# Identity and two pairs of q, k through SyncE; unit-matrix products that write PSUM with a step; table copies and a row read moved

## The chip, the cores and the metric

The kernel runs on one core of a Trainium2 chip. The metric is the device time of one execution in microseconds; the time given is the median of several runs. The core's engines are TensorE (PE: products, results to PSUM), VectorE (DVE), ScalarE (ACT), GpSimd (POOL) and SyncE (SP, which here only issues transfers). Each engine works its instructions off in the order of its own list and waits on semaphores in front of one whose operands aren't there. SyncE, ScalarE and GpSimd issue the DMA transfers.

## The reference

Windowed attention with eight global keys (4 batches, 8 heads, 768 positions, head width 64), then a block that mixes with two Fourier transforms, normalises and applies a two-layer perceptron:

```python
scores = scale * np.matmul(q, k.transpose(0, 1, 3, 2))
is_global = pos[None, :] < 8
is_local = (rel >= 0) & (rel < 96)
bias = -slopes[:, None, None] * dist[None, :, :]
a = softmax(where(is_global | is_local, scores + bias, -1e9))
attn = np.matmul(a, v)                       # 4 x 8 x 768 x 64
x = attn.transpose(0, 2, 1, 3).reshape(4, 768, 512)

mixed = np.real(fft(fft(x, axis=1), axis=2))
u = x + mixed
un = (u - mean(u)) / sqrt(var(u) + 1e-6)     # over the last axis
out = u + np.maximum(un @ w_ch1, 0.0) @ w_ch2
```

All inputs and the output are float32; the kernel computes in float16 with float32 sums.

## The kernel before

**Order.** The program is written as a list of units, and a planner (class `Plan`, L23) orders them when the kernel is built. Each unit names what it needs, the engine or engines that can do it, and a cost in us. The planner keeps a clock for each engine (`self.t`) and for two DMA streams ("DMA2": the first loads on SyncE and small constants; "DMA": the rest). It always takes the unit that could start first by these clocks; the table `BIAS` shifts chosen units or groups of units forward or back by a fixed number of us. TensorE's units come from four streams (MIX: transforms; ATT: attention; PH and PG: the perceptron's two layers), of which MIX and ATT may be taken up to ten places ahead. What comes out is a fixed order for every engine, and on the chip an engine waits wherever its next instruction is not ready. A queue of GpSimd has at most eight transfers on the way in the plan, as has SyncE's.

**Attention.** Heads are done in pairs, four pairs for a batch (`hp`, pair number n = 4b + hp). `load_qk` (L404) brings q and k of a pair: for batches 0 and 1 GpSimd issues a transfer that converts float32 to float16 on the way (L438); only pair 0 of batch 0 is read as float32 by SyncE (L426, tiles `u`) and converted by ScalarE or VectorE (`cast`, L443). `load_v` (L396) brings v by GpSimd. `trans` (L492) transposes q, then k on TensorE (L507, with the identity `idn` as the moving operand) and VectorE or ScalarE moves the result to `qkT` (L514, L518). `kg_copies` (L468) picks the global keys on GpSimd or VectorE. `score` (L525) makes three groups of scores for a pair; in batches 0 and 1 the distance bias is added by products of the table `dist` with a scaled identity `sid` (L549) ahead of the products of q and k (L559), and ScalarE takes the exponential out of PSUM (L583). Batches 2 and 3 instead multiply by tables `mk`, which ScalarE makes from `dist_k` (L1407); `dist_k` is two GpSimd copies of `dist` (L1403). In those batches q and k are transposed by DMA issued by SyncE (L485). `av` (L663) multiplies by v and normalises (L702, L704) into the tile X[b].

**Mixing.** `fold_0` (batch 0) and `fold_s`, `fold_d` form sums and differences on VectorE, with a scaling on ScalarE in batch 0 (`f5`, L812). `y_unit` (L900, four groups g) and `u_unit` (L985, three units of two row residues) are the two transforms on TensorE, `mirror` (L944) reversed copies on GpSimd. x itself must be added to u in another row order. In batches 1 to 3 `bounce` (L717) writes X[b] to a scratch tensor in DRAM (`xd`) and reads it back by rows (`xr`, L732); ScalarE issues both. In batch 0 `spread` (L988) adds x by 12 products of 64 x 64 tiles for each `u_unit` with shifted parts of a unit matrix (`PX`, L993), straight into the PSUM bank of u, whose columns are ordered by r, then n, where x has n, then r.

**Perceptron.** `nt_unit` (L1101) transposes the normalised rows, `ph_unit` (L1134, L1144) is the first layer, whose results ScalarE or VectorE moves to `hT` (L1150, L1151), `pg_unit` (L1157) the second; the last four tiles (c from 8) use seven products of quarter matrices in place of eight (`pg_units`, L1242). The rows leave by SyncE (L1182, L1345, L1349).

**Start.** The order in which the loads are listed begins at L1356: q and k of pair 0, the identity `ident`, `dist`, `gb` (all SyncE), q and k of pairs 2 and 1, v of pairs 0 and 2, q and k of pair 3, v of pairs 1 and 3, then batch 1 (all GpSimd). Twelve products on a zeroed tile (L1384) run on TensorE while nothing has landed.

Of the kernel before, what the change touches and what calls it, by code (L numbers as in the profile page):

```python
# [22 lines left out]
class Plan:  # L23
# [11 lines left out]
    def __init__(self):  # L35
        self.t = {"PE": 0.0, "ACT": 0.0, "DVE": 0.0, "POOL": 0.0, "SP": 0.7, "DMA": 3.75, "DMA2": 1.9}
        self.tok = {}
        self.ready = []
        self.pending = []
        self.rings = {}  # L40
        self.left = {}
        self.n = 0
        self.lanes = [0.0] * 8
        self.soft = [0.0] * 8
# [64 lines left out]
    def emit(self, place):  # L109
# [8 lines left out]
        if dma:  # L118
            q = "DMA2" if outs and outs[0] in (("ld", 0), ("ld", 1), ("c", "id"), ("c", "dist"), ("c", "gb")) else "DMA"
# [29 lines left out]
    def slot(self, tag):  # L149
# [7 lines left out]
    BIAS = {('mk1', '*', 4): 1.5, ('y', 1, 2, 2, 'r'): -3, ('qk', '*', 2): -0.7, (2, 90): -0.7, ('ob', '*', 2): -0.3,  # L157
            (3, '*', 7): -1.5, ('ex', 2, 2, 0): 1.5, ('ss', '*', 6): 0.3, (0, 20): -3, (1, 57): -0.7, ('mk1', '*', 5): 1.5,
            ('v', '*', 1): 1.5, ('c', 't2'): -0.3, ('mk1', '*', 7): 0.7, ('kG', '*', 1): 0.7, ('z', 1, 0): 3, ('u', 2, 0): 0.7}
# [4 lines left out]
    AQ = (4, 5)  # L164
    ORD = {("qk", 0): 0, ("v", 0): 0, ("qk", 1): 5, "w1": 6, "gate": 7, ("v", 1): 8, "w2": 9, ("qk", 2): 10, ("v", 2): 10, ("qk", 3): 10, ("v", 3): 10}
# [42 lines left out]
def act(n):  # L208
    return 0.06 + n / 1200.0


def dve(n):
    return 0.085 + n / 960.0
# [11 lines left out]
def kernel(  # L225
# [178 lines left out]
    def load_qk(b, hp):  # L404
# [3 lines left out]
        for w, src in enumerate((q, k)):  # L408
# [14 lines left out]
            if n == 0:  # L423
                def read(w=w, rows=rows):
                    t = stage["u", w] = buf("u", w, [P, 2 * NP, 2 * Dh], FP32, 1)
                    nc.sync.dma_start(t, rows)  # L426
                pl.later([("SP", 0.45, read)], [], 0.0, [("ld", w)], lat=1.7, dma=1.35)

                def cast(on, w=w):
                    place()  # L430
                    copy_on(on, qk16[n][:, w].rearrange("p h n t d -> p (h n) (t d)"), stage["u", w])
                pl.later([("ACT", act(768), lambda cast=cast: cast("ACT")), ("DVE", dve(768), lambda cast=cast: cast("DVE"))], [("ld", w)], 0.0,
                         [("qk", 0, w)], [("free", "u", w)], rank=0)
# [58 lines left out]
    def trans(b, hp):  # L492
# [6 lines left out]
        def run(start, ring):  # L499
# [9 lines left out]
            e = pl.pe(0.7, start, True)  # L509
# [15 lines left out]
    def score(b, hp, g):  # L525
# [3 lines left out]
        def run(start, ring):  # L529
# [33 lines left out]
            e = pl.pe(0.25 + 0.21 * pem, start, True)  # L563
# [153 lines left out]
    def bounce(b):  # L717
# [11 lines left out]
        def rd():  # L729
            XR[b] = buf("xr", b, [P, NS, Dm], FP16, 3)  # L730
            rows = XD[b].rearrange("(m r) d -> m r d", r=6)
            eng.dma_start(XR[b], rows)  # L732
        pl.later([("ACT", 0.5, rd)], [("xw", b)] + free("xr", b), 0.0, [("xr", b)], lat=1.7, dma=2.4)
# [58 lines left out]
    def fold_0():  # L792
# [19 lines left out]
        def f5(hp):  # L812
            pm = cell["pm"][:, hp]
            A(z(4, 1, hp)[:, 0], pm[:, 1, 0], AF.Copy, 0.0, c)
            A(z(5, 1, hp)[:, 0], pm[:, 0, 1], AF.Copy, 0.0, c)
# [19 lines left out]
        for x in range(2):  # L835
            for hp in (x, x + 2):
# [4 lines left out]
                pl.later([("ACT", 2 * act(128), lambda hp=hp: f5(hp))], [("f2", 0, hp)], 0.0, [("f5", 0, hp)], [("free", "ww", 0)], rank=0)  # L841
# [143 lines left out]
    def u_unit(b, pr):  # L985
        c = NP * b + pr

        def spread(pu):  # L988
            for jj in range(3):
                for a, r in enumerate(PAIRS[pr]):  # L990
                    for h in range(2):
                        t = slice(64 * (r % 2), 64 * (r % 2) + 64)
                        nc.tensor.matmul(pu[64 * h:64 * h + 64, a, :].rearrange("p (r n) -> p r n", r=4), PX[0][t, 3 * (r // 2) + jj],  # L993
                                         X[0][t, 3 * h + jj].rearrange("p (n r) -> p r n", r=4), start=(jj == 0), stop=False,
# [11 lines left out]
        def run(start, ring):  # L1006
# [28 lines left out]
            def add():  # L1035
                u = UT[c] = buf("u", c + 2, [P, 2, Dm], FP32, 2)
# [8 lines left out]
            def add1(on, a):  # L1045
                if a == 0:
                    UT[c] = buf("u", c + 2, [P, 2, Dm], FP32, 2)
# [6 lines left out]
            if b:  # L1054
                pl.later([("DVE", 2 * dve(512) + 0.25, add)], [("xr", b)] + free("u", c + 2), e, [("u", c, 0), ("u", c, 1)],
                         [("free", "xr", b)] + CD(b, ring), ring=ring)
            else:
                for a in range(2):
                    pl.later([("DVE", dve(512) + 0.06, lambda a=a: add1("DVE", a)), ("ACT", act(512) + 0.25, lambda a=a: add1("ACT", a))],
                             (free("u", c + 2) if a == 0 else [("us", c, 0)]), e, [("us", c, a)],  # L1060
# [498 lines left out]
```

## Time and profile before

| | |
|---|---|
| median of 5 runs | 263.2 us (262.88 to 266.57) |
| profiled execution | 263.45 us |
| its span, first to last instruction | 261.5 us |
| mean granted TensorE clock | 0.993 |
| PE busy | 246.1 us (94%) |
| DVE, ACT, POOL busy | 163.0, 143.0, 121.3 us |
| GpSimd's DMA queue (converting loads) | 66096 packets, 63.9% of 16 engines' span |
| first DMA queue of the other issuers | 24672 packets, 21.3% |

The page gives each engine's busy time and its share of the span. A timeline line has the start in us, the length, the engine, the line of the kernel, the operation, the tile written and the tiles read, and the number of instructions merged; in square brackets stands the idle time of the engine ahead of it and the work that ended it. A line of a stage has, after the stage's bounds, its length, then the busy time (and number of instructions) of PE, of PE's weight loads, DVE, ACT and POOL, the granted TensorE clock (1.00 is full), the DMA share and GB/s. A line of one source line has the shortest, median and longest duration in ns. SPq, ACTq and POOLq are instructions that issue transfers. A busy TensorE is not one at its peak, as ends of products are modelled.

### The profile page before, as it was taken

What the parts mean: (1) busy time and instruction counts of PE and PEld (TensorE: products, weight loads), DVE (VectorE), ACT (ScalarE), POOL (GpSimd) and SP (SyncE); (2) the same over time, 40 slices, a digit from 0 to 9 for tenths busy, and PEclk for the clock granted to TensorE, in tenths of its full rate; (3) what the DMA queues carried; (4) which work ended last, traced back from release to release, by engine and by line L of the source; (5) the groups of instructions that cost most, each with busy time, mean ns of one, the idle gap of its engine ahead of it and who ended that gap; (6) DMA issues with size and microseconds to landing.
All of it is one profiled execution on the core that took longest, in us unless ns stands there. A gap on an engine that the chain in (4) does not pass through costs nothing.

```text
span 261.5 us, 6774 instructions
## 1 busy us (share of the span) xinstructions
PE 246.1 (94%) x2824; PEld 178.9 (68%) x2824; DVE 163.0 (62%) x362; ACT 143.0 (55%) x240; POOL 121.3 (46%) x212
## 2 busy tenths in 40 slices
PE   7798879899969999999999999999999999999994
PEld 2576546589748676575477466588779568888883
DVE  1649995536981746712276977788986555625463
ACT  4198887675726697851055834794645236534300
POOL 8697796725928978899930304030304011010000
PEclk9799999999999999999999999999999999999999
DMA  7999999996999999999969941401450340200222
GB/s 166 179 158 175 273 206 119 101 202 85 146 139 228 153 136 142 130 127 119 120 117 166 176 190 39 125 3 43 96 188 0 83 120 0 85 38 3 80 83 80
DMA packets 93630, 31.52 MB, mean 121 GB/s; under 512 B 81664, under 2 KB 89984, under 8 KB 93600
## 3 DMA queue, kind: packets, MB, share of 16 engines
q0 software_dynamic: 66096, 14.18, 63.9%
q1 hardware_dynamic: 24672, 12.19, 21.3%
q10 hardware_dynamic: 2832, 4.72, 6.8%
q8 instruction: 22, 0.36, 0.6%
q14 instruction: 8, 0.07, 0.1%
HBM read 30.95 MB, written 8.65 MB: 151 GB/s over the span
## 4 chain that ended last, share of the span: by engine, by line
PE 53%; POOL 22%; DMA 18%; issue 2%; ACT 1%; DVE 1%; SPq 0%; ACTq 0%; POOLq 0%
PE ph L1144 20%; PE pg L1168 11%; POOL qk L414 10%; DMA qk<-in_q_dram 7%; POOL v L400 5%; PE pgD L1249 5%; PE pgA L1249 4%; DMA v<-in_v_dram 4%; PE pu L1017 4%; DMA hT<-in_k_dram 3%; PE py L914 3%; DMA qk<-in_k_dram 2%; DMA qkT<-qk 2%; POOL hT L438 2%; PE pav L685 2%
## 5 line engine op out<-in xcount | busy, mean ns | idle before, releaser
L1144 PE MATMUL ph<-unT,w 128*128 128x256 f16 x768 | 93.3, 273 | 3.4 <-ACT hT L1150 2.3
L1144 PEld LDWEIGHTS <-w 128*128 128x128 f16 x768 | 73.1, 98 | 16.7 <-issue 5.5
L1150 ACT ACTIVATE hT<-ph 128x512 f16<-128x512 f32 x83 | 48.9, 597 | 47.4 <-PE ph L1144 47.1
L1168 PE MATMUL pg<-w,hT 128*128 128x512 f16 x256 | 61.1, 379 | 0.0
L1168 PEld LDWEIGHTS <-hT 128*128 128x128 f16 x256 | 24.1, 98 | 23.7 <-issue 1.2
L1089 POOL TENSOR_SCALAR sm<-sm 128x2 f32<-128x2 f32 x12 | 3.0, 254 | 57.4 <-ACT un L1082 57.2
L400 POOL DMA_DIRECT2D v<-in_v_dram x32 | 24.7, 820 | 0.7 <-DMA hT<-in_k_dram 0.7
L583 ACT ACTIVATE ex<-sc 128x992 f16<-128x992 f32 (+2 forms) x24 | 20.6, 928 | 7.0 <-DVE qkT L514 5.7
L580 ACT ACTIVATE er<-sc 128x768 f16<-128x768 f32 (+2 forms) x24 | 21.5, 925 | 4.9 <-PE sc L555 4.0
L414 POOL DMA_DIRECT2D qk<-in_k_dram x32 | 21.4, 749 | 5.1 <-DMA qk<-in_k_dram 3.3
L414 POOL DMA_DIRECT2D qk<-in_q_dram x32 | 21.4, 730 | 4.1 <-DMA qk<-in_q_dram 2.4
L1177 DVE SCALAR_TENSOR_TENSOR u<-pg,sm,u 128x512 f32<-128x512 f32 x16 | 12.0, 750 | 18.0 <-PE pg L1168 18.0
L1073 ACT ACTIVATE un<-u,sm 128x512 f16<-128x512 f32 x17 | 11.8, 717 | 19.0 <-DVE sm L1043 17.5
L962 POOL COPY ww<-zy 128x512 f16<-128x512 f16 x16 | 9.7, 633 | 21.6 <-PE py L914 11.9
L595 DVE TENSOR_TENSOR ex<-er,mk 128x768 f16<-128x768 f16 (+2 forms) x24 | 15.8, 679 | 4.2 <-ACT er L580 4.2
L1039 DVE SCALAR_TENSOR_TENSOR u<-pu,xr 128x512 f32<-128x512 f32 x18 | 11.7, 688 | 9.6 <-PE pu L1017 9.6
L1082 ACT ACTIVATE un<-un 128x512 f16<-128x512 f16 x24 | 14.9, 624 | 4.7 <-DMA unT<-un 4.7
L685 PE MATMUL pav<-v,ex 128*128 128x65 f16 x352 | 16.9, 193 | 0.0
L685 PEld LDWEIGHTS <-ex 128*128 128x128 f16 x352 | 15.6, 97 | 0.8 <-issue 0.2
L473 POOL COPY kG<-qkT 64x8 f16<-64x8 f16 x28 | 8.5, 305 | 13.6 <-DMA qkT<-qk 12.6
L931 DVE CAST zy<-py 128x512 f16<-128x512 f32 (+1 forms) x8 | 7.1, 892 | 11.6 <-PE py L914 8.8
L929 ACT ACTIVATE zy<-py 128x1024 f16<-128x1024 f32 (+1 forms) x11 | 9.0, 829 | 9.1 <-PE py L914 6.1
(143 smaller groups left out, 390.3 us busy)
## 6 DMA issues: line engine op xcount, KB each, us to landing
out_dram<-u SPq DMA_DIRECT2D x23, 256.0 KB, 2.1
w<-in_moe_w_ch_dram POOLq DMA_DIRECT2D x8, 512.0 KB, 10.8
v<-in_v_dram POOLq DMA_DIRECT2D x32, 96.0 KB, 6.6
xr<-xd ACTq DMA_DIRECT2D x3, 768.0 KB, 4.5
qk<-in_q_dram POOLq DMA_DIRECT2D x32, 48.0 KB, 3.9
qk<-in_k_dram POOLq DMA_DIRECT2D x32, 48.0 KB, 3.5
xd<-x ACTq DMA_DIRECT2D x4, 384.0 KB, 4.6
hT<-in_q_dram POOLq DMA_DIRECT2D x5, 192.0 KB, 7.4
```

The source lines that it names most:

```text
L400: nc.gpsimd.dma_start(v16[b % 2][64 * t:64 * t + 64, h0:h0 + 2, :, 0:Dh].rearrange("m h i d -> m (h i) d"), v[b, h0:h0 + 2].rearrange("h ( ...
L414: nc.gpsimd.dma_start(qk16[n][64 * t:64 * t + 64, w, :, h], src[b, h0 + h].rearrange("(i m t) d -> t m i d", m=64, t=2)[t])
L580: A(mine(), cut(pa), AF.Exp, 0.0, 0.125)
L583: A(cut(expst[hp][:, :, g * 512:g * 512 + (384 if g == 2 else 512)]), cut(pa), AF.Exp, 0.0, 0.125)
L595: VT(o, mine(), m, op=ALU.mult)
L685: nc.tensor.matmul(o[:, s * 65:(s + 1) * 65], lhsT, v16[b % 2][:, 2 * hp + s, i, 0:65], start=(j < 2 and a == 0), stop=(a == len(ops) - 1) ...
L1082: A(x, x, AF.Square, accum_out=MV[c][:, a, 2:3])
L1144: nc.tensor.matmul(ph[:, a * CH:(a + 1) * CH].rearrange("p (x m) -> p x m", x=2), W1[0][:, d, jb * P:(jb + 1) * P], UNT[c][:, :, d, :], st ...
L1150: pl.later([("ACT", act(512), lambda: A(dst, ph, AF.Relu)), ("DVE", dve(512), lambda: V.tensor_scalar_max(dst, ph, 0.0))], [], e, [("h", c ...
L1168: nc.tensor.matmul(pg, HT[c][:, jb, t * P:(t + 1) * P], W2[0][:, jb, :], start=(jb == 0), stop=(jb == NJ - 1))
L1177: V.scalar_tensor_tensor(UT[c][:, t, :], pg, MV[c][:, t, 3:4], UT[c][:, t, :], op0=ALU.mult, op1=ALU.add)
L1249: nc.tensor.matmul(o, lhs(j), rhs(j), start=(first and j == 0), stop=(j == NK - 1), skip_group_check=True)
```

## The change

- SyncE's list begins with the identity, then q and k of pair 0, `dist`, q and k of pair 2, `gb`. q and k of pair 2 of batch 0 are read as float32 and converted by ScalarE or VectorE, as those of pair 0; GpSimd no longer loads them. The `u` tiles of the tail shift by two numbers more (`U0` = 4), as four of them serve the loads first.
- `spread`: x is now read in its own order (n, then r, contiguous), and the result is written to PSUM with a step of 128 words.
- The two `dist_k` copies wait for the last sum of u's third tile (`("us", 2, 1)`) instead of the last x of batch 0.
- The row read of x (`rd`) is issued by SyncE instead of ScalarE.
- `f5` may run on ScalarE or on VectorE.
- Nine warm-up products instead of twelve.
- The list has the first unit of u after the first two groups of y in all batches (before: ahead of y in batch 0, behind y and the mirror copies in the others).
- The planner has other costs for ScalarE, VectorE, transposes, scores, other first clocks of the two DMA streams, and a new table of biases.

```diff
-        self.t = {..., "SP": 0.7, "DMA": 3.75, "DMA2": 1.9}
+        self.t = {..., "SP": 0.7, "DMA": 6.6, "DMA2": 1.2}
...
-    BIAS = {('mk1', '*', 4): 1.5, ('y', 1, 2, 2, 'r'): -3, ('qk', '*', 2): -0.7, (2, 90): -0.7, ('ob', '*', 2): -0.3,
...
+    BIAS = {('u', '*', 1): -1.5, (1, 63): 0.7, ('w', '*', 2): -0.7, ('un', '*', 0): -1.5, (3, '*', 7): -1.5, ('qkT', 14): -3,
+            ('ex', 0, 3, 1): 0.7, ('qk', 9, 0, 1): -0.3, ('w2', '*', 1): 0.3, ('ld', '*', 1): -1.5, (3, '*', 1): -3, ('xw', 3): -3,
...
+    HW = (0, 2)
+    U0 = 4
...
 def act(n):
-    return 0.06 + n / 1200.0
+    return 0.1 + n / 1180.0
 def dve(n):
-    return 0.085 + n / 960.0
+    return 0.13 + n / 960.0
...
-            if n == 0:
+            if n in pl.HW:
                 def read(w=w, rows=rows):
-                    t = stage["u", w] = buf("u", w, [P, 2 * NP, 2 * Dh], FP32, 1)
+                    t = stage["u", n, w] = buf("u", w + n, [P, 2 * NP, 2 * Dh], FP32, 1)
                     nc.sync.dma_start(t, rows)
...
-            e = pl.pe(0.7, start, True)
+            e = pl.pe(1.0, start, True)
...
-            e = pl.pe(0.25 + 0.21 * pem, start, True)
+            e = pl.pe(0.27 + 0.28 * pem, start, True)
...
-            eng.dma_start(XR[b], rows)
-        pl.later([("ACT", 0.5, rd)], [("xw", b)] + free("xr", b), 0.0, [("xr", b)], lat=1.7, dma=2.4)
+            nc.sync.dma_start(XR[b], rows)
+        pl.later([("SP", 0.5, rd)], [("xw", b)] + free("xr", b), 0.0, [("xr", b)], lat=1.7, dma=2.4)
...
-        def f5(hp):
+        def f5(hp, on):
             pm = cell["pm"][:, hp]
-            A(z(4, 1, hp)[:, 0], pm[:, 1, 0], AF.Copy, 0.0, c)
-            A(z(5, 1, hp)[:, 0], pm[:, 0, 1], AF.Copy, 0.0, c)
+            for i, w in ((4, pm[:, 1, 0]), (5, pm[:, 0, 1])):
+                if on == "ACT":
+                    A(z(i, 1, hp)[:, 0], w, AF.Copy, 0.0, c)
+                else:
+                    V.tensor_scalar_mul(z(i, 1, hp)[:, 0], w, c)
...
-                        nc.tensor.matmul(pu[64 * h:64 * h + 64, a, :].rearrange("p (r n) -> p r n", r=4), PX[0][t, 3 * (r // 2) + jj],
-                                         X[0][t, 3 * h + jj].rearrange("p (n r) -> p r n", r=4), start=(jj == 0), stop=False,
+                        nc.tensor.matmul(pu[64 * h:64 * h + 64, a, :].rearrange("p (r n) -> p n r", r=4), PX[0][t, 3 * (r // 2) + jj],
+                                         X[0][t, 3 * h + jj].rearrange("p (n r) -> p n r", r=4), start=(jj == 0), stop=False,
...
+        dma_const(ident, id_d, 0.3, ("c", "id"))
         load_qk(0, 0)
-        dma_const(ident, id_d, 0.3, ("c", "id"))
         dma_const(dist_sb, dist_d, 0.75, ("c", "dist"))
+        if 2 in pl.HW:
+            load_qk(0, 2)
         dma_const(gb_sb, gb_d, 0.1, ("c", "gb"))
-        load_qk(0, 2)
+        if 2 not in pl.HW:
+            load_qk(0, 2)
         load_qk(0, 1)
...
-        for _ in range(12):
+        for _ in range(9):
             nc.tensor.matmul(pz[:, 0, :], EG[:, 0:P], EG, start=True, stop=True)
...
-                     [("c", "dist")] + ([("ex", 0, 3, 2)] if any((0, hp) in DM for hp in range(HP)) else [("x", 0, 3, 1)]), 0.0, [("dk", t)], rank=3)
+                     [("c", "dist")] + ([("us", 2, 1)]), 0.0, [("dk", t)], rank=3)
...
-            if b == 0:
-                u_unit(b, 0)
-            for g in (0, 1, 2, 3):
+            for g in (0, 1):
+                y_unit(b, g)
+            u_unit(b, 0)
+            for g in (2, 3):
                 y_unit(b, g)
             mirror(b)
-            if b:
-                u_unit(b, 0)
             u_unit(b, 1)
```

## The prediction

> **What bounds the kernel now.** I read the page's busy times first, then TensorE's stages, then the places where it stood still, then the start of each queue. The profiled execution took 263.45 us, of which the span is 261.5; 1.95 us lie around it. The median of the five runs is 263.2, so a sum made against this execution is lowered by 0.25 at the end.
>
> ```profile
> PE 246.1 (94%) x2824; PEld 178.9 (68%) x2824; DVE 163.0 (62%) x362; ACT 143.0 (55%) x240; POOL 121.3 (46%) x212
> ```
>
> TensorE is busy for all but 15.4 us. Stages show where those lie:
>
> ```profile
> 0.00:7.70 7.70, 5.00 (x13) 1.64 (x13) 1.17 (x10) 2.97 (x3) 6.66 (x17) 1.00 0.82 177
> 7.70:50.50 42.80, 36.90 (x749) 25.10 (x750) 31.79 (x102) 32.17 (x47) 34.75 (x55) 0.96 1.68 171
> 50.50:75.50 25.00, 25.00 (x340) 20.29 (x341) 16.61 (x34) 15.27 (x32) 12.74 (x23) 1.00 1.13 140
> 75.50:77.80 2.30, 0.04 (x1) 0.00 (x0) 2.27 (x4) 1.25 (x3) 0.61 (x2) 1.00 2.44 134
> 77.80:258.00 180.20, 179.05 (x1724) 131.89 (x1723) 110.70 (x216) 91.30 (x157) 66.55 (x119) 1.00 0.72 103
> ```
>
> The first pair after the stage is its length and TensorE's busy time. The first 7.70 us hold no useful product (the 5.00 are warm-up products on a zeroed tile). Up to 50.5 another 5.9 us are idle; then TensorE is full to the end, but for one hole of 2.29 us at 75.5 and 1.15 us in 180. So the time is TensorE's work plus the idle time of the first 78 us: whatever takes idle time out there, or work out anywhere, moves the end one for one, as long as data for the later batches keep up. The start, and the hole:
>
> ```profile
> 7.89 0.86 PE L507 MATMUL pt<-ident,hT 128*64 128x128 f16 x24
> 9.14 0.85 PE L507 MATMUL pt<-ident,hT 128*64 128x128 f16 x12 [0.39 <-DMA hT<-in_q_dram]
> 10.22 0.85 PE L507 MATMUL pt<-ident,hT 128*64 128x128 f16 x12 [0.23 <-DMA hT<-in_k_dram]
> ...
> 66.40 1.34 ACTq L725 DMA_DIRECT2D xd<-hT  x2
> 76.15 0.35 ACTq L732 DMA_DIRECT2D xr<-xd  x1
> 76.55 0.74 ACT L1407 ACTIVATE mk<-distk 128x640 f16<-128x640 f16 x1 [4.56 <-DMA xd<-hT]
> ...
> 77.82 1.91 PE L1144 MATMUL ph<-unT,w 128*128 128x256 f16 x16 [2.29 <-ACT hT L1150]
> ```
>
> Pair 0 waits for the identity, pair 2 for its k; and at 72 us ScalarE stands for 4.56 us, its queue held by the row read of x (L732) until the write of x has landed, so no ph bank is emptied and TensorE runs dry.
>
> **1. Row read of x by SyncE.** The issue (0.35 us, three times) leaves ScalarE, and the 4.56 us of waiting go to SyncE. TensorE's 2.29 us hole had no other cause: ScalarE's mk tables and hT evacuations behind it were ready. Gain 2.3. Behind the read on SyncE stand a store of out (73.83 before) and the transposes of qk (78.62, which waited for qk data anyway), so it has 2.5 us of room there. For batch 2 it stands among four transposes that fill SyncE from 139.0 to 148.0; the writes' landing took up to 9.0 us, and a transpose held by it would delay scores of batch 3. TensorE has pg products of earlier rows to run meanwhile, so 0; up to 1 us lost if the cover is gone.
>
> **2. Start: order on SyncE, two loads moved.** By the new list of biases k of pair 0 is issued first (a bias of -1.5 on ("ld", 1)), then identity, q of pair 0, dist, q and k of pair 2, gb, at some 0.5 us each (rows of 0.43 to 0.54). The first load landed for ScalarE at 4.23 before and the second at 5.55; with 64 KB of identity between them, the second would be 5.8, its cast (0.84) ends at 6.65, and the first transposes start there rather than at 7.89: 1.2 earlier. The identity is there at about 4.5, so sid (1.16 us of VectorE) and the sums of ones are done before. Pair 0's scores began at 11.0, because in TensorE's queue pair 2's transposes stood ahead; they now need dist, which landed at 8.8 (issued 2.40, 6.4 to landing).
>
> Pair 2 is the doubtful part. Its k must land on SyncE's queue behind dist. At the pace of the second load behind the first (1.32 us each) it lands at 8.8 + 2.64 = 11.4; cast, transposes (0.86) and evacuation (0.96) bring its first exponential to 14.5, where it was at some 14.7 (ScalarE's six from 12.09 on, 0.84 each). So nothing is lost there and little won. Best case: it lands at 9.4, as the plan's own figures have it (a start of 1.2, four loads at 1.35, identity and dist 1.05, 1.7 to be seen), and the exponentials run on from pair 0's at 9.9 instead of 12.09: 2.2 won. Worst case: identity and dist, 384 KB, took from 5.55 to 8.8, 118 KB per us beside GpSimd's loads; 768 KB at that pace land at 15.3, and the first exponential of pair 2 is at 18.5, 3.8 late.
>
> GpSimd drops two issues (0.83 each) and two converting loads, which landed 1.08 apart (9.13 and 10.21); v and pair 3 come some 2.2 earlier. ScalarE waited 0.62 and 0.18 us for pair 3's scores (at 20.66 and 21.83); those waits go. With 0.2 from pair 2 (14.5 for 14.7) the start gives 1.0; the best case above makes it 3.0, the worst -3.8. Two casts of 0.84 more lie in ScalarE's idle time (6.4 to 12.1); without that cover they cost 1.7.
>
> The Trainium skill (DMA: Bandwidth & Descriptors, "Issuing engines are not separate DMA queues") says that transfers issued by different engines share the same 16 engines, so that another issuer saves only issue time. By it the moved loads would arrive no sooner than before, and the start would keep only the identity's share; no row here shows pair 2 in SyncE's queue.
>
> **3. Tables later.** The dist_k copies held GpSimd from 30.01 to 33.62, with kG copies behind them, for which TensorE waited 0.93 us at 38.54. They go behind u of the third tile (about 50), where GpSimd is idle for 1.71 and 2.07 us; the mk tables need them at 68.3 only. VectorE's last fold ended at 38.63, beside the end of that wait, so I count half: 0.5 (0 to 0.9). If the later place were not free, rstd would be 3.6 late; its first user on VectorE stood at 73.05, so nothing follows.
>
> **4. Products with the unit matrix (L993).** 36 products, nine steps of four at a time. They now read x with a step of four elements:
>
> ```profile
> L993 PE MATMUL pu<-x,er x36: 607/626/646, 31.9 to 47.3; 64*64 64x512 f16 x36
> 44.17 1.35 PE pu L993 x12
> 31.01 0.40 PE L549 MATMUL sc<-dist,sid 64*64 64x496 f16 x4
> ```
>
> A step of four takes 0.45 us (12 in 1.35). Four score products of 496 columns, plain on both sides, took 0.23 (31.01 to the next at 31.24). After the change the read is plain and the write to PSUM has a step of 128 words; no matmul of the trace writes so. If the write is free, nine steps save 9 x 0.22 = 2.0. If it is as slow as the stepped read: 0. VectorE reads PSUM with this very step at 0.69 us for 512 (L1053); at that pace four take 0.69 and nine lose 2.2. I take 0, by the nearest row, the same instruction with one of its sides stepped.
>
> The Trainium skill (PSUM — Partial Sum Buffer, "Specifications (TRN2)") has lines of 8 bytes in PSUM and says that any pattern that isn't contiguous slows matmuls significantly. By it the change gains nothing here or loses; the trace's stepped read shows a factor of two for SBUF, and nothing for PSUM.
>
> **5. The rest.** Three warm-up products fewer (0.43 us apart) end at 4.9 rather than 6.2, in idle time. The records show the clock halved from 9.1 to 12.5 after the idle stretch before 7.7; a longer one could halve pair 0's transposes, 0.86 more: kept for the range. A half of the fold's scaling may go to VectorE (0.3 us each, eight in all), y and u change places in the list, and new costs and biases move the whole order: 0, with 1.5 either way, as the holes of this order (0.2 to 1.1 us each up to 50.5) show what a misplaced item costs.
>
> Sum: 2.3 + 1.0 + 0.5 + 0 = 3.8. 263.45 - 3.8 = 259.65 for such an execution, **259.4** against the median.
>
> **Rivals.**
> (a) The stepped write runs at the plain rate: 2.0 more, 257.4. For it: VectorE's stepped read of PSUM costs no more than its plain one (0.69 for both L1053 and L1151). Against it: 0.69 per 512 is too slow a test for 0.22.
> (b) The hole is closed, the start isn't shortened: pair 2 lands near 13, the casts stand in ScalarE's way, or TensorE waits later for batch 2 or 3, whose loads form the chain from 62.6 to 146. Then 2.3 less about 0.8: 261.7, which is no change.
> (c) Slower: SyncE's share of the DMA engines. k of pair 2 at 15.3 holds all exponentials of batch 0 up by 3.8, since TensorE's and ScalarE's queues are in order, and 2.3 + 0.5 come back: 263.2 + 1.0 = 264.2, with the order's 1.5 up to 265.7. It decides from a landing at 14.4 (11.6 keeps pair 2's old time, 2.8 later eats the other gains). For it: 118 KB per us. Against: the first loads' 1.32 us each, and two loads fewer on GpSimd's queue.
> (d) That the moved loads don't leave GpSimd is excluded: the diff issues them on SyncE.
>
> **How the numbers follow.** Forecast 0.40, (a) 0.28, (b) 0.18, (c) 0.14. A measurement of this kernel can tell about 1% (2.6 us) from no change, that is below 260.6 or above 265.8. The forecast and (a) are below it but for order's 1.5 (0.66 in all, with a little of (b)); (b) and most of (c) lie within: 0.24; a tenth is left above, (c) with a bad order or a slow PSUM write beside it. The likeliest case's own range is 257.9 to 260.9, the order's 1.5 either way; to hold most of (a) with a better start (257.4 less up to 2.0) and (c), the range is 255.8 to 264.5.
>
> **What would show it.** First transposes at 6.6 to 6.8; pair 2's k cast at 11 to 12.5 (at 16: (c)); no wait of ScalarE for xd and no hole near 75; L993 at 12 in 1.35 (0.7: (a); 2 or more: the write is slow); pgl before the y products without GpSimd ahead of it; TensorE full from 48 on. Wrong, if the hole comes back elsewhere, or idle time past 78 us grows by more than 1.5.

## The result, and the profile after

The changed kernel takes 263.91 us (median of 38 runs, 262.38 to 265.61) where the kernel before takes 263.11 (64 runs beside it). The ratio is 1.0036, 95% interval 1.0022 to 1.0050: 0.6 to 1.3 us slower, no gain. The ratios, here and below, leave out executions in a second, slower state, so they differ a little from the quotients of the medians. The profiled execution of the changed kernel took 263.31, its span 261.5, as long as that of before. On the chip SyncE's order is k of pair 0, the identity, q of pair 0, `dist`, q and k of pair 2, `gb`: the biases put k ahead of the identity, and q of pair 0 comes third.

TensorE's busy time (page, part 1), and its stages in the trace of the changed kernel, cut at the same times as before; the first pair is the stage's length and TensorE's busy time, and the last three numbers are the granted clock, the DMA share and GB/s:

```profile
PE 246.9 (94%) x2821; PEld 180.6 (69%) x2821; DVE 167.4 (64%) x374; ACT 139.8 (53%) x234; POOL 119.7 (46%) x206
```

```profile
0.00:7.70 7.70, 4.11 (x17) 1.36 (x17) 2.97 (x21) 2.12 (x2) 6.66 (x17) 1.00 0.86 193
7.70:50.50 42.80, 35.58 (x667) 24.77 (x668) 27.54 (x87) 31.00 (x41) 26.06 (x43) 0.88 1.56 176
50.50:75.50 25.00, 24.59 (x388) 19.50 (x386) 20.12 (x44) 19.66 (x42) 17.37 (x28) 1.00 1.40 188
75.50:77.80 2.30, 2.30 (x20) 1.68 (x18) 1.39 (x3) 1.42 (x3) 2.30 (x4) 1.00 1.05 272
77.80:258.00 180.20, 180.18 (x1739) 133.25 (x1736) 114.79 (x220) 85.62 (x148) 67.33 (x118) 1.00 0.67 95
```

Read them from the bottom. The hole at 75.5 is gone (2.30 busy of 2.30, before 0.04), and of the 1.15 us of idle time behind it 0.02 are left. Yet the span is no shorter: from 7.7 to 50.5 TensorE is busy for 1.32 us less than before, and the work that was not done there comes later. In the first 7.7 us it has 0.89 less, but that is warm-up products. Some of what is busy is also slower: the granted clock of the second stage is 0.88, before 0.96. The first y products begin 4.87 us later (kernel before, then changed kernel):

```profile
38.86 2.14 PE L914 MATMUL py<-t,ww 128*128 128x256 f16 x18
```

```profile
43.73 1.92 PE L922 MATMUL py<-t,ww 128*128 128x256 f16 x16
```

So the hole was closed and the start got longer. The list of ScalarE in time order (start, length, instruction, in brackets the idle time before it and what ended it), and the transposes on TensorE that wait for it:

```profile
3.83 0.84 ACT L448 ACTIVATE hT<-u 128x768 f16<-128x768 f32 x1 [1.82 <-DMA u<-in_k_dram]
8.50 0.84 ACT L448 ACTIVATE hT<-u 128x768 f16<-128x768 f32 x1 [3.83 <-DMA u<-in_q_dram]
11.40 0.84 ACT L448 ACTIVATE hT<-u 128x768 f16<-128x768 f32 x1 [2.06 <-DMA u<-in_q_dram]
13.96 0.84 ACT L448 ACTIVATE hT<-u 128x768 f16<-128x768 f32 x1 [1.72 <-DMA u<-in_k_dram]
14.71 2.64 ACT L588 ACTIVATE ex<-sc 128x992 f16<-128x992 f32 x3
```

```profile
9.39 1.49 PE L512 MATMUL pt<-ident,hT 128*64 128x128 f16 x24 [4.10 <-ACT hT L448]
...
13.30 0.85 PE L512 MATMUL pt<-ident,hT 128*64 128x128 f16 x12
14.86 0.85 PE L512 MATMUL pt<-ident,hT 128*64 128x128 f16 x12 [0.70 <-ACT hT L448]
```

The four casts (L448, before L443) wait for k and q of pair 0, then q and k of pair 2. Pair 0's q is there at 8.50, not at 5.8, so the first transposes start 1.50 later than before instead of 1.2 earlier, though the identity has landed by 4.11 (its first use, on VectorE). Pair 2's k is there at 13.96. And the first exponential stands **behind** its cast in ScalarE's list: pair 0's first scores are written by 12.6 (products at 11.94, 0.63 long), and their exponentials begin at 14.71 (12.09 before). The chain of waits names the same transfer, issued as the sixth on SyncE, as its longest piece:

```profile
3.35 10.58 DMA u<-in_k_dram
13.96 0.85 ACT hT L448
14.86 0.85 PE pt L512 x6
```

The row read is where it was meant to be, on SyncE (SP's list), with ScalarE emptying ph banks through the place of the old hole:

```profile
70.95 0.34 SPq L737 DMA_DIRECT2D xr<-xd  x1
71.59 1.32 SPq L490 DMA_TRANSPOSE qkT<-qk  x1
```

```profile
75.23 0.60 ACT L1158 ACTIVATE hT<-ph 128x512 f16<-128x512 f32 x1 [0.40 <-PE ph L1152]
76.11 0.60 ACT L1158 ACTIVATE hT<-ph 128x512 f16<-128x512 f32 x1 [0.28 <-PE ph L1152]
```

And the unit-matrix products (L1001, before L993), shortest, median and longest in ns, and twelve of them in a row:

```profile
L1001 PE MATMUL pu<-x,er x36: 586/631/631, 36.4 to 52.1; 64*64 64x512 f16 x36
48.33 1.42 PE pu L1001 x12
```

### The profile page after: what moved, and what is told of

The parts are those of the page before. It is cut to its first block, busy times and chain, and to the rows that moved or that the text cites. A ratio compares the mean times of both kernels' runs of the same rounds, so it can differ in the third digit from the quotient of the medians.

```text
span 261.5 us, 6768 instructions
## 1 busy us (share of the span) xinstructions
PE 246.9 (94%) x2821; PEld 180.6 (69%) x2821; DVE 167.4 (64%) x374; ACT 139.8 (53%) x234; POOL 119.7 (46%) x206
## 4 chain that ended last, share of the span: by engine, by line
PE 83%; DVE 5%; ACT 4%; DMA 4%; issue 1%; SPq 1%; DVEq 0%
PE ph L1152 33%; PE pg L1176 21%; PE pgD L1257 5%; PE pgA L1257 4%; DMA u<-in_k_dram 4%; PE pu L1025 4%; PE py L922 4%; PE pav L690 4%; PE sc L560 3%; ACT ex L588 2%; PE pav L682 1%; DVE x L709 1%; PE pt L512 1%; PE sc L554 1%; PE pgl L644 1%
## 5 line engine op out<-in xcount | busy, mean ns | idle before, releaser
L1176 PEld LDWEIGHTS <-hT 128*128 128x128 f16 x256 | 24.2, 98 | 23.9 <-issue 1.3
L405 POOL DMA_DIRECT2D v<-in_v_dram x32 | 26.7, 886 | 5.1 <-DMA hT<-in_k_dram 3.0
L585 ACT ACTIVATE er<-sc 128x992 f16<-128x992 f32 (+2 forms) x24 | 21.5, 929 | 10.9 <-DVE ex L600 7.4
L600 DVE TENSOR_TENSOR ex<-er,mk 128x992 f16<-128x992 f16 (+2 forms) x24 | 15.1, 643 | 16.3 <-ACT er L585 16.3
L419 POOL DMA_DIRECT2D qk<-in_k_dram x32 | 23.6, 938 | 1.2 <-DMA w<-in_moe_w_ch_dram 0.9
L419 POOL DMA_DIRECT2D qk<-in_q_dram x32 | 22.8, 904 | 0.0
L970 POOL COPY ww<-zy 128x512 f16<-128x512 f16 x16 | 11.8, 765 | 18.7 <-PE py L922 18.7
L1081 ACT ACTIVATE un<-u,sm 128x512 f16<-128x512 f32 x11 | 7.9, 720 | 18.4 <-DVE sm L1051 17.3
L682 PE MATMUL pav<-vG,eg 128*128 128x130 f16 x64 | 12.6, 220 | 1.2 <-DVE x L709 0.5
L1257 PEld LDWEIGHTS <-hT 128*128 128x128 f16 x128 | 12.5, 98 | 1.6
L519 DVE COPY qkT<-pt 128x1536 f16<-128x1536 f16 x6 | 5.7, 956 | 11.5 <-PE pt L512 11.5
```

Of the source, the lines that this page charges most:

```text
L405: nc.gpsimd.dma_start(v16[b % 2][64 * t:64 * t + 64, h0:h0 + 2, :, 0:Dh].rearrange("m h i d -> m (h i) d"), v[b, h0:h0 + 2].rearrange("h ( ...
L419: nc.gpsimd.dma_start(qk16[n][64 * t:64 * t + 64, w, :, h], src[b, h0 + h].rearrange("(i m t) d -> t m i d", m=64, t=2)[t])
L585: A(mine(), cut(pa), AF.Exp, 0.0, 0.125)
L600: VT(o, mine(), m, op=ALU.mult)
L682: nc.tensor.matmul(o.rearrange("p (h d) -> p h d", d=65), EG[:, (j - 2) * P:(j - 1) * P], vG[b % 2][:, 2 * hp:2 * hp + 2, 0:65], start=Tru ...
L1176: nc.tensor.matmul(pg, HT[c][:, jb, t * P:(t + 1) * P], W2[0][:, jb, :], start=(jb == 0), stop=(jb == NJ - 1))
```

## The theories and the experiments

**Theory S** (start): the row read gains, and pair 2's way through SyncE loses as much or more, since SyncE's transfers from the third on arrive late beside GpSimd's converting loads and ScalarE's list has the casts ahead of the exponentials. Rivals: **C**, the lower clock at the start; **W**, the stepped write; **P**, the new order of the plan, apart from the loads; **G**, the closed hole is given back by later transfers. Every ratio below is to the kernel before as it ran beside that run, with its 95% interval; the median of before was 262.8 to 264.3 us there, so runs are compared by their ratios and not by their times. The changed kernel stands at 1.0036.

### One part each way: the row read

In the kernel before (`b_rowread_sync`), and taken back in the changed kernel (`a_rowread_scalar`):

```diff
-            eng.dma_start(XR[b], rows)
+            nc.sync.dma_start(XR[b], rows)
```

> The kernel before, with the row read of x issued by SyncE in place of ScalarE, nothing else. Theory S (the change closes ScalarE's hole and loses as much at the start): the 2.29 us hole at 75.5 goes and nothing takes it back, 260.8 to 261.3. Rival G (time won in the middle is given back later, by the loads of batches 2 and 3): the hole goes, idle time after 78 us grows by as much, 262.7 to 263.3.

Measured: 0.9945 (0.9916 to 0.9975), 261.91 us. The stages from 75.5 on, and the one new wait of TensorE:

```profile
75.50:77.80 2.30, 2.30 (x20) 1.86 (x19) 2.27 (x4) 0.89 (x3) 2.30 (x4) 1.00 1.01 262
77.80:258.00 180.20, 177.15 (x1708) 130.01 (x1705) 110.52 (x217) 90.09 (x155) 63.60 (x115) 1.00 0.73 101
```

```profile
88.44 0.34 PE L555 MATMUL sc<-qkT 64*128 64x256 f16 x4 [1.20 <-DMA qkT<-qk]
```

The hole is closed (what the second line leaves idle is 1.8 us of waits and 1.2 behind TensorE's last product, which ends 1.3 us sooner than before). The scores of batch 2 then wait 1.20 us for the transposes of qk, which stand behind the row read in SyncE's list: the first of them went out at 67.52 before and goes out at 74.89 here, after the read at 74.32. 1.45 us of 2.3 are kept (0.55% of 263.1; the interval has 0.25 to 0.84%). G holds in part, for this order.

> The kernel after, with the row read of x issued by ScalarE again at the same point of the order. Theory S: ScalarE waits 3 to 4 us for the write of x near 67 us, a hole of 1.5 to 2.5 us on TensorE comes back, 265.4 to 266.3. Rival G: no change, 263.5 to 264.3.

Measured: 1.0102 (1.0042 to 1.0162), 265.44 us in 6 runs, 263.72 to 267.67. So the read is worth 0.66% in the changed kernel too, about 1.7 us, with a wide interval (0.04 to 1.28%). The hole that S expected isn't in the trace: ScalarE issues the read at 70.36 without a long wait, and nothing stands at 75.5. The profiled execution was the fastest of the six, and where the slower ones lose the time isn't shown.

### W and C: the write and the clock

The unit-matrix products as before, in the changed kernel (`a_plain_write`):

```diff
-   pu[...].rearrange("p (r n) -> p n r", r=4), ..., X[0][...].rearrange("p (n r) -> p n r", r=4)
+   pu[...].rearrange("p (r n) -> p r n", r=4), ..., X[0][...].rearrange("p (n r) -> p r n", r=4)
```

> The kernel after, with the unit-matrix products reading x with a step and writing PSUM plainly, as before. All theories that leave the products out: no change, 263.5 to 264.3, a product 626 ns and twelve in 1.35 to 1.45 us. Rival W (the stepped write costs more than the stepped read): twelve take 0.2 to 0.7 us less, 261.8 to 263.4.

Measured: 1.0047 (1.0009 to 1.0085), the same as the changed kernel (0.1% apart, within 0.4), and 626 ns for a product. The stepped write costs what the stepped read costs; W falls.

28 warm-up products instead of 9 (`a_warm28`):

```diff
-        for _ in range(9):
+        for _ in range(28):
```

> The kernel after with 28 warm-up products in place of 9, which fill TensorE until about 9.3. Rival C (the start is lost because the granted clock is halved from 8.5 to 18.3 us): the clock stays full, the first exponentials come 1 us sooner and the time falls by 1.5 to 2.5, to 261.4 to 262.4. Theory S (the start waits for pair 0's q at 8.5 and pair 2's k at 14.0 in ScalarE's list): the clock stays full, the first exponential stays at 14.7, the time falls by 0 to 0.8: 263.1 to 263.9.

Measured: 1.0071 (1.0028 to 1.0114), not faster. The granted clock is 1.00 throughout, pair 0's transposes take 0.86 rather than 1.49, but the warm-ups end at 10.2, so that the transposes start at 10.33; the first exponential is at 14.92, since pair 2's k decides it and not TensorE. The y products came 1.3 us sooner, and the lead was lost further on: 1.04 us of idle time stand at 55.92, for which the trace shows no wait (0.34 at 57.22 in the changed kernel), and 1.11 at 103.08:

```profile
103.08 1.03 PE L1152 MATMUL ph<-unT,w 128*128 128x256 f16 x8 [1.11 <-DVE hT L1159]
```

VectorE's copy of hT is late there behind a step on two columns (L1051) that took 1.63 us in this trace and 0.17 in that of the changed kernel; why isn't shown. The executions of the changed kernel say the same of C: 12 had a mean clock of 0.99 or more and a median of 263.6, and 25 had less than 0.985 and 264.0. By this the clock goes with some 0.4 us, which the spread of either group (some 3 us) doesn't make certain, and not with the 4.5 between forecast and result.

### Which load is late: the order on SyncE

In the changed kernel q of pair 0 second and the identity third (`a_q_before_ident`); in the kernel before the identity first, then q, and k of pair 0 third (`b_ident_first`). The reads themselves are unchanged, only exchanged in SyncE's list (the first kernel's edit; the second's is like it):

```diff
+                    if (n, w) == (0, 0):
+                        nc.sync.dma_start(ident, id_d.ap())
+                    else:
+                        load()
...
-        dma_const(ident, id_d, 0.3, ("c", "id"))
+        pl.later([("SP", 0.45, lambda: LOAD[0, 0]())], [], 0.0, [("c", "id")], lat=1.6, dma=0.3)
```

> The kernel after; on SyncE the second and third transfers change places (k, q of pair 0, then identity), all else in the same order. Theory S (what SyncE issues third, at 1.8 us, lands among GpSimd's loads): q lands near 5.6 and is cast by 6.4, the identity near 7.7, the first transposes start at 7.8 in place of 9.39; pair 2's k still holds the exponentials at 14.0 to 14.7, so the time falls by only 0 to 0.8. Rival (the third is late because of its size): the identity, a sixth of q's size, lands by 6.0 and the first transposes start at 6.5.

Measured: 1.0018 (0.9988 to 1.0048), not told apart from the changed kernel. Now q's cast is at 5.42 and the identity is what TensorE waits for, at the first sums of ones:

```profile
8.12 0.28 PE L1442 MATMUL pones<-one,ident 128*32 128x1 f16 x8 [3.37 <-DMA ident<-idm]
```

> The kernel before with identity, q, k in this order on SyncE in place of q, k, identity; nothing else. Theory S (what is issued third, at 1.8 us, lands near 8): q is cast from 4.5, k lands near 7.8 in place of 5.5, the transposes of pair 0's k start at 8.7 to 9.2, pair 2's follow at 9.5 and 10.3 as before; 263 to 264, no gain from the identity. Rival (as the prediction had it): k lands at 5.8, the first transposes start at 6.6 and the time falls by up to 1.

Measured: 0.9987 (0.9945 to 1.0029), no gain. q's cast is at 4.54, and k's, third, at 7.33, where it was 5.55 as the second. So the third transfer of SyncE is there at 8.50 (384 KB of q), 8.12 (64 KB of identity) or 7.33 (384 KB of k). All traces in which GpSimd's loads run from the start agree: the third is first used at 6.63 to 8.10 us where it is the identity (four traces) and at 7.33 to 8.74 where it is a load of 384 KB (seven). These overlap; among GpSimd's loads a sixth of the size doesn't make the third early. Moving the identity ahead buys nothing, because something else is then third.

### Pair 2 out of SyncE's list, and its cast off ScalarE

In the changed kernel pair 2 comes by GpSimd's converting loads again, first in its list and ahead of pair 1, without casts (`a_pair2_gpsimd`); the rest of the order stays:

```diff
+                def load(w=w, rows=rows):
+                    ...
+                    nc.gpsimd.dma_start(qk16[n][:, w].rearrange("p h n t d -> p (h n) (t d)"), rows)
+                LOAD[n, w] = load
...
+            if n == 1:
+                run = lambda w=w: LOAD[2, w]()
```

> The kernel after with q and k of pair 2 loaded by GpSimd ahead of pair 1's, as before, and without their casts; the order of everything else is that of the kernel after. Theory S: pair 2 is there at 9 to 10.5, the first exponential of pair 0 comes at 12.8 in place of 14.7, the y products start 1.5 to 2 us sooner than 43.7, and the time falls by 1 to 2, to 262 to 263. Rival P (the plan's new order costs the start, whatever the loads): the y products stay at 43 to 44 and the time within 0.5 of the kernel after.

Measured: 0.9952 (0.9921 to 0.9983), 262.8 us: 0.84% under the changed kernel (0.50 to 1.18, the two intervals put together), 2.2 us. ScalarE's first exponential, by its list:

```profile
8.62 0.84 ACT L463 ACTIVATE hT<-u 128x768 f16<-128x768 f32 x1 [3.63 <-DMA u<-in_q_dram]
12.74 1.86 ACT L603 ACTIVATE ex<-sc 128x992 f16<-128x992 f32 x2 [3.28 <-PE sc L579]
```

It is 1.97 us earlier than in the changed kernel. The y products, at 43.23, are only 0.5 earlier, which I had not expected and which was P's sign; the time is S's. The profiled execution took 263.69 and was one of the slowest of its twelve (261.24 to 263.81), so the trace doesn't show where the 2.2 us lie. 0.9952 is also what the row read alone gives (0.9945): beside the row read and pair 2, **all other parts of the change together measure nothing that these runs can tell** (0.07% apart, within 0.43%, which is 1.1 us).

The cast of pair 2's k on VectorE instead (`a_cast_vector`):

```diff
-   copy_on(on, qk16[n][:, w]..., stage["u", n, w])
+   copy_on("DVE" if n and w else on, qk16[n][:, w]..., stage["u", n, w])
```

> The kernel after with the cast of pair 2's k on VectorE in place of ScalarE, nothing else. Theory S (pair 0's exponentials stand behind this cast in ScalarE's list): the first exponential comes at 12.8 in place of 14.7; pair 2 is no sooner, so ScalarE waits for it instead, and the time falls by 0.3 to 1. If ScalarE's list is not what holds the start: no change.

Measured: 1.0023 (0.9990 to 1.0056), not told apart from the changed kernel (0.1% under it, within 0.4). ScalarE's first exponentials:

```profile
12.41 1.84 ACT L588 ACTIVATE ex<-sc 128x992 f16<-128x992 f32 x2
16.41 0.81 ACT L588 ACTIVATE ex<-sc 128x768 f16<-128x768 f32 x1 [2.15 <-PE sc L564]
```

The first comes at 12.41, but the third, also pair 0's (128x768), waits 2.15 us: its scores stand behind pair 2's transposes in TensorE's list, and these wait for k, cast on VectorE at 14.10. Pair 2's own then wait another 1.58. One wait takes the place of the other, so the late landing counts, more than where the cast stands.

### Who makes the loads late

GpSimd's first converting load (issued at 1.23) waits until k of pair 0 has landed, by a copy of one column of it; nothing else is changed (`a_gpsimd_held`):

```diff
+                if (n, w) == (1, 0):
+                    hold = kon.tile([P, 1], FP32, tag="hold", name="hold")
+                    nc.gpsimd.tensor_copy(hold, stage["u", 0, 1][:, 0, 0:1])
```

> The kernel after; GpSimd's first load waits until pair 0's k has landed (a copy of one column, 3.9 us in place of 1.2), all its loads come 2.7 us later. Theory S (GpSimd's loads share the engines and hold up SyncE's third to sixth transfer): q of pair 0 is cast from 5.6 to 6.4 in place of 8.5 to 9.3 and the first transposes start near 6.5; pair 2's k lands at 10 to 12 in place of 14.0. Rival (SyncE's transfers are slow by themselves): q still lands at 8 to 8.5. The time itself can go either way, since v and pairs 1 and 3 come later: 262.5 to 266.

Measured: 0.9876 (0.9825 to 0.9927), 260.95 us in 4 runs. ScalarE's list, then TensorE's:

```profile
6.80 0.84 ACT L451 ACTIVATE hT<-u 128x768 f16<-128x768 f32 x1 [1.88 <-DMA u<-in_q_dram]
9.55 0.84 ACT L451 ACTIVATE hT<-u 128x768 f16<-128x768 f32 x1 [1.91 <-DMA u<-in_q_dram]
10.93 0.84 ACT L451 ACTIVATE hT<-u 128x768 f16<-128x768 f32 x1 [0.53 <-DMA u<-in_k_dram]
11.68 1.84 ACT L591 ACTIVATE ex<-sc 128x992 f16<-128x992 f32 x2
```

```profile
7.69 1.49 PE L515 MATMUL pt<-ident,hT 128*64 128x128 f16 x24 [2.28 <-ACT hT L451]
```

With the same list on SyncE and GpSimd's load 3.0 us later (4.23), q of pair 0 is there 1.70 us earlier, pair 2's k 3.03 earlier, and the kernel is 1.6% faster than without the hold (1.1 to 2.1), better than I had expected. Single traces bear this out: where pair 2 comes by SyncE, its k is there at 13.96 to 14.94 in the seven without a hold and at 9.86 to 10.93 in the four with one. So GpSimd's loads delay SyncE's third and later transfers. They are not the whole delay of q: it is at 6.80, not at the 5.6 expected, and what holds it there isn't shown. y begins at 40.21. P falls: the order is the changed one. Nor is it the clock, which reads 1.00 here: the changed kernel's own executions at 0.99 or more had a median of 263.6.

The hold together with q second and identity third (`a_held_q_second`), that is, both of these edits:

```diff
+                    nc.gpsimd.tensor_copy(hold, stage["u", 0, 1][:, 0, 0:1])
...
-        dma_const(ident, id_d, 0.3, ("c", "id"))
+        pl.later([("SP", 0.45, lambda: LOAD[0, 0]())], [], 0.0, [("c", "id")], lat=1.6, dma=0.3)
```

> The kernel after with GpSimd's first load held until pair 0's k has landed, and with q of pair 0 second and the identity third on SyncE. Theory S: pair 0's casts end at 6.3, the identity lands by 6.8, the first transposes start at 6.8 in place of 7.7 (held alone) and 9.39 (after); 260.0 to 260.9, a ratio of 0.983 to 0.988 to before. If the first transposes don't matter because pair 2's k (11 us) holds the exponentials: as held alone, 260.7 to 261.3.

Measured: 0.9878 (0.9824 to 0.9933), 259.43 us, by the ratio the same as the hold alone (within 0.75%). The identity is there at 5.6 and the transposes start at 6.28, in 0.86 rather than 1.49, behind 0.40 us of idle time:

```profile
6.28 0.86 PE L523 MATMUL pt<-ident,hT 128*64 128x128 f16 x24 [0.40 <-ACT hT L459]
```

First exponential 10.99 (11.68 with the hold alone), y at 40.18 (40.21): something other than pair 0's start sets y here. Five warm-ups more in it (`a_held_q_second_warm`):

```diff
-        for _ in range(9):
+        for _ in range(14):
```

> As the kernel with GpSimd held and q second, with 14 warm-up products in place of 9, which end near 6.3. The clock then stays full at the first transposes (twelve tiles of pair 0 in 0.43 us in place of 0.75). Theory S: the first exponential of pair 0 comes 0.5 to 1 sooner, but pair 2's k holds the rest: 0 to 0.6 less than with 9. Rival C: 1 to 2 less.

Measured: 0.9925 (0.9897 to 0.9953): full clock (0.998 against 0.986), first exponential at 10.61, y at 40.01, and no gain: 0.5% above the same with nine, within 0.6. C falls here too. 1.4 us of idle time stand between 50.5 and 75.5 (0.3 with nine).

The hold in the kernel before, with the row read on SyncE, until q of pair 0 has landed (`b_rowread_held`):

```diff
+                if (n, w) == (2, 0):
+                    LOAD[0]()                # the read of q of pair 0, first on SyncE as before
+                    ...
+                    nc.gpsimd.tensor_copy(hold, stage["u", 0][:, 0, 0:1])
```

> The kernel before with the row read of x on SyncE and GpSimd's first load, which here is pair 2, held until pair 0's q has landed. Theory S (holding helps because it frees SyncE's transfers, and pair 2 must be one of those): the identity lands 1 to 1.5 sooner than 7.7, pair 2 comes 2 to 2.7 later than 10.2, the scores of pair 0 start no sooner; 262 to 264, slower than with the row read alone (261.9). Rival Q (holding GpSimd helps whatever it loads): 259.5 to 261.

Measured: 1.0013 (0.9984 to 1.0042), 0.7% slower than the row read alone. Pair 0's transposes start at 6.61, but pair 2, which comes by the held loads there, has its k only at 10.65, and the exponentials after pair 0's wait 1.27 us. The granted clock also stays halved longer, to 16.7 us (13.1 with the row read alone); how much of the loss is the clock's isn't shown. The hold isn't good in itself; it helps where pair 2 doesn't come by GpSimd. Rival Q falls.

### Pair 2's move alone, in the kernel before

The runs above take pair 2's move out of the changed kernel only; they leave open whether it makes the loss by itself. Row read on SyncE and pair 2 through SyncE behind `dist`, in before's order (`b_rowread_pair2`), and the same with GpSimd held until q of pair 0 has landed (`b_rowread_pair2_held`):

```diff
-        dma_const(dist_sb, dist_d, 0.75, ("c", "dist"))
+        pl.later([("SP", 0.45, lambda: (nc.sync.dma_start(dist_sb, dist_d.ap()), PAIR2["load", 0](), PAIR2["load", 1]()))], ...)
...
+                    PAIR2["cast", 0](); PAIR2["cast", 1]()    # behind pair 0's second cast
...
+                    nc.gpsimd.tensor_copy(hold, stage["u", 0][:, 0, 0:1])    # the held one only
```

> The kernel before with two parts of the change: the row read of x on SyncE (alone 0.9945 of before) and q, k of pair 2 by SyncE, issued behind the distance table, their two casts on ScalarE behind pair 0's. Everything else stays in before's order. Theory S (pair 2's way through SyncE is what the change loses): k of pair 2 lands at 13 to 15, the first exponential is at 14 to 15.5 rather than 12.1, and the time is 1.000 to 1.005 of before, 0.6 to 1.0 per cent above the row read alone. Rival P (the rest of the changed order costs the time, pair 2 is hidden): within 0.3 per cent of the row read alone, 0.992 to 0.997. GpSimd's first load comes behind its memsets here, some 0.7 us later than in the changed kernel, which could bring pair 2 up to 1 us earlier.

Measured: 1.0118 (1.0051 to 1.0184), 265.76 us in 6 runs, 1.7% above the row read alone (1.0 to 2.5). ScalarE's list:

```profile
14.43 0.84 ACT L460 ACTIVATE hT<-u 128x768 f16<-128x768 f32 x1 [1.71 <-DMA u<-in_k_dram]
17.20 2.56 ACT L600 ACTIVATE ex<-sc 128x992 f16<-128x992 f32 x3 [1.93 <-DVE qkT L531]
```

The loss is there, larger than S had it. In before's order pair 0's scores stand behind pair 2's transposes on TensorE, so k's landing at 14.43 holds up everything, and the first exponential is 5.1 us later than in the kernel before. The changed plan had put pair 0's first scores ahead (10.81 in its trace), and its first exponential was 2.6 later: the new order **softened** the loss, the opposite of P.

> The same, and GpSimd's first converting load waits by a copy of one column until q of pair 0 has landed, at about 4. Theory S: pair 0's and pair 2's loads have the transfers to themselves, k of pair 2 lands near 10.9 and the first exponential is at 11.5 to 12; the time is 0.985 to 0.992 of before, below the row read alone. Rival P (holding helps only together with the changed order): no faster than the row read alone, 0.9945 or above, as the same hold was 1.0013 with pair 2 on GpSimd.

Measured: 1.0002 (0.9964 to 1.0040), 262.53 us: 1.2% faster than without the hold (0.4 to 1.9), again from earlier landings (pair 2's k at 10.26), but not the 0.985 to 0.992 of S; P's figure, 0.9945 or above, was the nearer one. The first exponential is at 13.03, for the same reason: pair 0's scores follow pair 2's transposes at 11.16.

```profile
10.26 0.84 ACT L464 ACTIVATE hT<-u 128x768 f16<-128x768 f32 x1 [0.48 <-DMA u<-in_k_dram]
13.03 2.56 ACT L604 ACTIVATE ex<-sc 128x992 f16<-128x992 f32 x3 [1.93 <-DVE qkT L535]
```

So with pair 2 on SyncE the hold helps in either order, and of the two only the changed order came below the row read alone.

TensorE's busy time in the first 20 us shows these starts side by side: kernel before, changed kernel, changed kernel held, and `b_rowread_pair2`, in this order (the second number after the window is its busy time, the clock is the third number from the end):

```profile
0.00:20.00 20.00, 16.18 (x270) 10.09 (x270) 8.27 (x32) 10.88 (x13) 16.59 (x31) 0.91 1.72 168
```

```profile
0.00:20.00 20.00, 13.37 (x166) 7.66 (x167) 7.18 (x30) 8.38 (x10) 13.69 (x26) 0.74 1.51 186
```

```profile
0.00:20.00 20.00, 15.64 (x237) 9.10 (x238) 9.70 (x32) 11.93 (x15) 14.55 (x27) 1.00 1.52 190
```

```profile
0.00:20.00 20.00, 11.31 (x144) 6.43 (x148) 5.94 (x26) 7.21 (x8) 13.68 (x27) 0.74 1.43 177
```

The changed kernel has done 2.8 us less by 20 us (1.1 of it warm-ups) and `b_rowread_pair2` 4.9 less. The sum closes: the row read takes 1.45 us off, pair 2 puts 2.2 on, which makes 0.75 where 0.6 to 1.3 were measured. Either term is uncertain by some 0.8 us, and the sum is the comparison of 0.9952 with 0.9945 over again, not a second proof; the second one is `b_rowread_pair2`.

## Why the prediction was wrong, step by step

**The step that failed** is part 2, the start, which was to give 1.0; pair 2's move in it cost 2.2 (1.3 to 3.1), and the identity's place gave nothing clear. Two sentences of it were wrong. "With 64 KB of identity between them, the second would be 5.8": it was 8.50. I had read the gap between SyncE's first two loads (1.32 us) as the price of a load by its size; but those two stand ahead of most of GpSimd's traffic, and amid that traffic the third place in the list is late with 64 KB as with 384. The row that showed this stood in the trace of before: the identity, third there, was issued at 1.82 and first used at 7.67, which I took for the price of its place behind two large loads. "At the pace of the second load behind the first (1.32 us each) it lands at 8.8 + 2.64 = 11.4": it was 13.96; the pace among GpSimd's loads was 2.56 between pair 2's q (11.40) and k. The bound from the other side, 118 KB per us, gave 15.3 and was nearer.

Rival (c) had the mechanism and nearly the time (264.2 for 263.9), with a landing of 14.4 as the point from which it decides. That the time is so near is partly luck: the landing was 13.96 and not 15.3, and by (c)'s own sum that costs 2.4 (13.96 less 11.6) against gains of 2.8 and makes 262.8. The landing hurt more than the working had it, because that asked only when pair 2's exponentials would run. Pair 0's work stands behind pair 2's as well: its exponentials behind the cast in ScalarE's list, which rival (b) called casts in ScalarE's way, and its third scores behind pair 2's transposes on TensorE. `a_cast_vector` takes the first away, and the second takes its place. That the two together make up the rest is argued; no run takes both away and leaves the landing.

**The row read**: the mechanism was right and the size was off. 2.3 were counted, 1.45 kept in before's order and some 1.7 in the changed one. The transposes behind it on SyncE, which I gave room of 2.5 us, held scores of batch 2 for 1.20 at 88.4 in `b_rowread_sync`. The room was read from the transposes at 78.62, and the one at 67.52, which the read also holds up in that order, was left out; the "up to 1 us lost" was kept for batch 3. In the changed kernel this wait doesn't occur.

**The tables**, 0.5: the wait of pgl behind GpSimd is gone from the trace, but what is left of the change without the row read and pair 2 measures 0.9952 to 0.9945. A gain of 0.5 us (0.2%) can't be excluded there, and isn't shown.

**The stepped write**, 0: right, by the same row that was taken for it (631 ns for 626). **Warm-ups** in idle time: right. **The clock**, kept for the range at 0.86: halved from 8.3 to 18.5 us, before from 9.1 to 12.5, worth some 0.4 if anything.

**The order**, 1.5 either way: the new one left 0.02 us of idle time after 77.8; that this is a gain isn't shown, as the late start had pushed work there. With all else that was changed, beside the row read and pair 2, it measures within 1.1 us of nothing.

The signs named for "wrong" were only half met: the idle time past 78 us didn't grow, and the hole did come back, at the front.

The Trainium skill (DMA: Bandwidth & Descriptors, "Issuing engines are not separate DMA queues") says that transfers of all issuers interleave on the same 16 DMA engines, and that another issuer saves the issue time only. The runs agree: moved from GpSimd to SyncE, pair 2's k is there at 13.96, where TensorE had it at 10.22 before, and holding GpSimd's loads brings it to 10.93.

## What to carry to other kernels

Price a moved load by its place in the list and by what other queues have under way then, not by the gap between the first two loads; if a load has to be early, changing its issuer alone can make it later; holding back the competing queue made it earlier here, as long as nothing that is needed first comes by that queue (with pair 2 on GpSimd the hold cost 0.7%). A cast that waits for a load holds all that stands behind it on its engine, so ask which other work waits there, not only that load's own users. When a hole far from the start is closed, look whether the start still feeds TensorE early enough; the held version, 1.2% faster than before, does both.

## What the runs showed of the hardware

Three things I had not expected. Beside GpSimd's loads the third transfer on SyncE took about as long with 64 KB (issued at 1.83, used at 8.12) as with 384 KB (1.82 and 8.50); with these loads held back the size did count (64 KB used at 5.48 to 5.68 in four traces, 384 KB at 6.80 in one). A product that writes PSUM with a step of 128 words runs as slowly as one that reads SBUF with a step of four (631 and 626 ns). And the granted clock in the records doesn't tell all: in `a_gpsimd_held` it reads 1.00 for all stages, yet pair 0's 24 transposes, behind 2.28 us of idle time, took 1.49 us; behind 0.40 us, in `a_held_q_second`, they took 0.86.

Open are why `a_warm28` and `a_held_q_second_warm` have more idle time between 50.5 and 75.5, most of it with no wait in the trace, and how `a_pair2_gpsimd` gains 2.2 us with y only 0.5 earlier.

The Trainium skill (PSUM — Partial Sum Buffer, "Specifications (TRN2)") says that a pattern in PSUM that isn't contiguous slows matmuls significantly; the runs agree and give it a size here: twelve stepped writes follow each other in 1.42 us, 0.47 for four, where four plain products of 496 columns took 0.23.
